# Retiming two short stretches of a TensorE-bound kernel: the first attention chunk and the second batch's numerators

**Chip, cores, metric.** One core of a Trainium2 chip (trn2). The metric is the device time of one execution in microseconds (us).

## The reference

Linear attention with cosine weights, then a multiplicative feed-forward network (FFN) without a nonlinearity:

```
B, H, S, D = 8, 8, 576, 64
phi(x) = concat(relu(x) * cos_w, relu(x) * sin_w)       # 128 features
kv  = einsum('bhsf,bhsd->bhfd', phi(k), v);   z = sum_s phi(k)
num = einsum('bhsf,bhfd->bhsd', phi(q), kv);  den = einsum('bhsf,bhf->bhs', phi(q), z) + 1e-6
x   = (num / den) as [4608, 512]
out = ((x @ w1) * (x @ w2)) @ w3 @ w_out                # FFN width 1024
```

## The kernel before

The kernel folds w3 @ w_out into one matrix (w34b), goes through nine tiles of 512 tokens, and puts the attention of coming batches between the FFN's matmuls, in numbered slots. The order of the program is the order on each engine; nothing is reordered later. Around batch 1 a slot is mostly four FFN matmuls of 512 columns long, 0.86 us.

In outline, an attention chunk of 128 rows goes: features (cosine half on VectorE, sine half on ScalarE), transposes of q on TensorE into PSUM, the memory that matmuls write (`q_tr`), a copy to `qpT`, numerator and denominator matmuls into PSUM tile `pnum` (`num`; they need `kvs`, the copy of the batch's kv sums), normalisation on VectorE into `xblk`, transposes of it (`x_tr`), and a copy to `xT`, which the FFN reads. Batches 0 and 1 transpose `xblk` on TensorE, later batches by DMA.

```python
ps_att = tile_pool(name="ps_att", bufs=1, space=PSUM)     # pnum: one buffer
ps_tr  = tile_pool(name="ps_tr",  bufs=2, space=PSUM)     # pst: two buffers

def num(b, c):
    nt = ps_att.tile([P, 2, 512], FP32, name="pnum")      # (batch 0, chunk 0 has its own, pfirst)
    for h in range(H):                                     # numerator and denominator, 65 columns
        nc.tensor.matmul(nt[:, h // 4, ...], lhsT=qpT[:, h, ...], rhs=kvs[:, h, :], ...)
    nc.vector.tensor_scalar_add(out=den, in0=n4[..., 64], scalar1=1e-6)
    nc.vector.reciprocal(out=den, in_=den)
    nc.vector.tensor_tensor(out=xblk, in0=n4[..., 0:D], in1=den..., op=ALU.mult)

def x_tr(b, c):                                            # (batches 0 and 1)
    pst = ps_tr.tile([P, 8, 128], BF16, name="pst")
    for kc in range(4):
        nc.tensor.transpose(pst[:, kc, 0:R], xf[:, ts(kc, 128)], identb[rows, rows])
    nc.scalar.copy(out=xT[t][:, :, ds(o, R)], in_=pst[:, 0:4, 0:R])

def idle_mms(n): ...    # n matmuls of zeros into PSUM tile "unread", read by nobody: fillers

# start, after the k features and v copies of batch 0; kv_first() has two steps, matmuls and copies
idle_mms(31)                       # issued at the very start
...
next(kv_steps); prep_q(0, 0); next(kv_steps); prep_q(0, 1)
idle_mms(2)
q_tr(0, 0); prep_q(0, 2); q_tr(0, 1, evac=False)[1](); num(0, 0)
...                                # idle_mms(3), x_tr(0, 0), num(0, 1), q_tr(0, 2), first FFN matmuls

# batch 1: the slot of each chunk's kv matmuls, q transposes, numerator, output transposes
spread(prep_units(1, (prep_q,)), 13, 15, between)
spread(prep_units(1, (prep_v,)), 15, 16, between)
attention_at(1, between, kv=(16, 16, 17, 17, 18), tr=(14, 15, 15, 16, 17),
             nu=(19, 20, 21, 22, 24), xt=(20, 21, 22, 23, 25))
```

## Time and profile before

| | before |
|---|---|
| time, median (range) | 263.0 us (262.46 to 263.11) |
| span of the profiled run | 261.2 us |
| TensorE (PE) busy | 249.4 us, 96% |
| granted TensorE clock | 0.997 |
| q's first part lands | 11.38 us |
| first FFN matmul | 16.60 us |
| transpose of batch 0's chunk 3 | 22.31 us |
| first matmul of the second tile | 67.51 us |

With TensorE at 96% only two things can be won: its idle time, and filler matmuls that hide idle time. The prediction shows the lines that place both: the start, up to 22 us, and batch 1's attention, 50 to 70 us. Losses on TensorE are counted from start to start, a matmul's real start against the earliest start that the matmuls before it allow; the wait view shows about 0.17 us less for each.

### The profile page before, as it was taken

What the parts mean: (1) busy time and instruction counts of PE and PEld (TensorE: products, weight loads), DVE (VectorE), ACT (ScalarE), POOL (GpSimd) and SP (SyncE); (2) the same over time, 40 slices, a digit from 0 to 9 for tenths busy, and PEclk for the clock granted to TensorE, in tenths of its full rate; (3) what the DMA queues carried; (4) which work ended last, traced back from release to release, by engine and by line L of the source; (5) the groups of instructions that cost most, each with busy time, mean ns of one, the idle gap of its engine ahead of it and who ended that gap; (6) DMA issues with size and microseconds to landing.
All of it is one profiled execution on the core that took longest, in us unless ns stands there. A gap on an engine that the chain in (4) does not pass through costs nothing.

```text
span 261.2 us, 5061 instructions
## 1 busy us (share of the span) xinstructions
PE 249.4 (96%) x1939; PEld 135.2 (52%) x1972; DVE 144.6 (55%) x344; ACT 128.4 (49%) x219; POOL 85.2 (33%) x146
## 2 busy tenths in 40 slices
PE   8989999998799999999999999999999999999992
PEld 2568555474365456545544654464455444444441
DVE  6877544466669827852883497178616613413320
ACT  2766324746765574555655565546533233323321
POOL 7744144440742177036604920430050031022000
PEclk9999999999999999999999999999999999999998
DMA  7999999999769399999998999835591453014015
GB/s 196 182 193 204 208 204 202 198 199 204 194 84 181 75 193 159 180 143 192 182 187 170 159 190 144 166 98 97 115 173 41 43 110 90 0 34 129 0 45 120
DMA packets 68025, 37.11 MB, mean 142 GB/s; under 512 B 35616, under 2 KB 64544, under 8 KB 68000
## 3 DMA queue, kind: packets, MB, share of 16 engines
q0 software_dynamic: 35488, 27.20, 64.9%
q1 hardware_dynamic: 32352, 9.44, 22.0%
q8 instruction: 15, 0.25, 0.4%
q10 hardware_dynamic: 160, 0.13, 0.2%
q14 instruction: 10, 0.08, 0.1%
HBM read 38.80 MB, written 9.44 MB: 185 GB/s over the span
## 4 chain that ended last, share of the span: by engine, by line
PE 91%; DVE 4%; ACT 1%; issue 1%; ACTq 0%
PE ffnps L399 46%; PE ffnps L445 21%; PE ffnps L208 5%; PE pnum L316 4%; PE pst L298 4%; PE unread L168 4%; PE pnum L267 3%; DVE xblk L323 2%; PE pst L196 1%; PE pst L345 1%; DVE den L321 1%; DVE den L320 1%; PE ffnps L462 0%; ACT kvs L272 0%; ACT osb L464 0%
## 5 line engine op out<-in xcount | busy, mean ns | idle before, releaser
L438 DVE TENSOR_TENSOR abT<-asb,ffnps 128x512 bf16<-128x512 bf16 x68 | 46.4, 683 | 65.8 <-PE ffnps L399 65.2
L399 PE MATMUL ffnps<-xT,w1b 128*128 128x512 bf16 (+2 forms) x312 | 74.2, 357 | 1.2 <-ACT xT L346 0.7
L399 PE MATMUL ffnps<-xT,w2b 128*128 128x512 bf16 (+2 forms) x306 | 73.2, 357 | 0.5
L434 ACT CAST asb<-ffnps 128x512 bf16<-128x512 f32 x68 | 39.8, 585 | 64.1 <-PE ffnps L399 56.7
L445 PE MATMUL ffnps<-w34b,abT 128*128 128x512 bf16 x272 | 63.4, 379 | 0.4
L384 POOL DMA_DIRECT2D out_dram<-osb x42 | 22.3, 536 | 120.0 <-ACT osb L451 119.9
L399 PEld LDWEIGHTS <-w1b 128*128 128x128 bf16 x320 | 28.8, 97 | 27.6 <-issue 0.8
L445 PEld LDWEIGHTS <-abT 128*128 128x128 bf16 x280 | 26.5, 98 | 30.1 <-DVE abT L438 0.4
L399 PEld LDWEIGHTS <-w2b 128*128 128x128 bf16 x320 | 27.4, 97 | 22.5
L451 ACT COPY osb<-ffnps 128x512 f32<-128x512 f32 x35 | 20.5, 585 | 37.8 <-PE ffnps L445 36.7
L243 ACT ACTIVATE qp<-qs,sinv 128x512 bf16<-128x512 bf16 (+1 forms) x40 | 28.3, 720 | 1.7 <-DMA qs<-in_q_dram 1.7
L323 DVE TENSOR_TENSOR xblk<-pnum,den 128x512 bf16<-128x512 f32 (+1 forms) x39 | 26.9, 691 | 1.3
L243 ACT ACTIVATE kp<-ks,sinv 128x512 bf16<-128x512 bf16 (+1 forms) x35 | 24.8, 721 | 0.0
L316 PEld LDWEIGHTS <-qpT 128*128 128x128 bf16 x320 | 15.1, 98 | 8.6 <-DVE xblk L323 0.9
L259 POOL COPY va<-vs 128x512 bf16<-128x512 bf16 (+1 forms) x30 | 18.4, 638 | 0.0
L300 DVE COPY qpT<-pst 128x1024 bf16<-128x1024 bf16 (+1 forms) x22 | 13.7, 626 | 8.0 <-PE pst L298 7.6
L316 PE MATMUL pnum<-kvs,qpT 128*128 128x65 bf16 x312 | 16.4, 194 | 0.1
L240 DVE TENSOR_SCALAR qp<-qs,cosv 128x512 bf16<-128x512 bf16 (+1 forms) x40 | 16.2, 413 | 0.6 <-DMA qs<-in_q_dram 0.6
L267 PEld LDWEIGHTS <-kp 128*128 128x128 bf16 x280 | 12.9, 98 | 5.4
L298 PE MATMUL pst<-identb,qp 128*128 128x128 bf16 x192 | 14.5, 219 | 0.6 <-ACT qp L243 0.4
L208 PE MATMUL ffnps<-woutb,w3T 128*128 128x512 bf16 x62 | 14.9, 379 | 0.1
L298 PEld LDWEIGHTS <-qp 128*128 128x128 bf16 x192 | 12.2, 98 | 5.2 <-ACT qp L243 1.2
(73 smaller groups left out, 178.0 us busy)
## 6 DMA issues: line engine op xcount, KB each, us to landing
out_dram<-osb POOLq DMA_DIRECT2D x16, 256.0 KB, 3.6
out_dram<-osb POOLq DMA_DIRECT2D x24, 128.0 KB, 3.1
qs<-in_q_dram POOLq DMA_DIRECT2D x9, 256.0 KB, 7.8
ks<-in_k_dram POOLq DMA_DIRECT2D x7, 320.0 KB, 8.0
qs<-in_q_dram POOLq DMA_DIRECT2D x7, 320.0 KB, 8.4
vs<-in_v_dram POOLq DMA_DIRECT2D x7, 320.0 KB, 9.9
w3b<-in_moe_w_dram POOLq DMA_DIRECT2D x8, 256.0 KB, 13.3
ks<-in_k_dram POOLq DMA_DIRECT2D x7, 256.0 KB, 8.9
```

The lines of the kernel that those rows point to most:

```text
L208: nc.tensor.matmul(acc[:, :], lhsT=w3T[:, lc, :], rhs=woutb[:, lc, :], start=(lc == 0), stop=(lc == 7))
L243: nc.scalar.activation(out=dst[:R, c, :, D:F], in_=src[:R, :, c, :], func=ACTF.Relu, scale=sinv[:R, at:at + 1], bias=0.0)
L267: nc.tensor.matmul(kvt[:, h // 4, ds((h % 4) * 65, 65)], lhsT=kp[:, c, h, :], rhs=va[:, c, h, 0:D + 1], start=(i == 0 and h % 4 == 0), sto ...
L298: nc.tensor.transpose(pst[:, h, :], qp[:, c, h, :], identb[:])
L316: nc.tensor.matmul(nt[:, h // 4, ds((h % 4) * 65, 65)], lhsT=qpT[:, h, ds(at, 128)], rhs=kvs[:, h, :], start=True, stop=True)
L323: nc.vector.tensor_tensor(out=xblk[rows], in0=n4[:, :, :, 0:D], in1=den[rows].unsqueeze(3).to_broadcast([R, 2, 4, D]), op=ALU.mult)
L384: on.dma_start(out=rows[:, :, cols], in_=osb[64 * i:64 * i + rows.shape[0], :, cols])
L399: nc.tensor.matmul(out, lhsT=w[:, kc, ts(jc, 128)], rhs=x[:, kc, tok], start=(kc == 0), stop=(kc == 3))
L434: nc.scalar.copy(out=asb[:], in_=aT[:, :])
L438: nc.vector.tensor_mul(out=abT[:, jc, :], in0=asb[:], in1=bT[:, :])
L445: nc.tensor.matmul(ops[:, :], lhsT=abT[:, jc, ts(ms, 128)], rhs=w34b[:, jc, :], start=(jc == 0), stop=(jc == 7))
L451: nc.scalar.copy(out=osb[:, ms % 2, :], in_=ops[:, :])
```

## The change

Its intent: at the start, shorten the chain from q's arrival to the first FFN matmul (half of chunk 0's sine on VectorE, two output copies on VectorE, another order, fewer fillers). In batch 1, prepare q and v earlier, and put output transposes two slots after their numerators, so that TensorE need not wait for the normalisation.

```diff
-    idle_mms(31)
+    idle_mms(27)
@@ features(): sine on ScalarE for the first `scalar_heads` heads, the others on VectorE
@@ kv_first(): both copies of kvs on ScalarE (was one on ScalarE, one on VectorE)
@@ num(): chain=False returns the normalisation, to be issued later
@@ x_tr(): by_vector=True has the copy on VectorE
-    prep_q(0, 0)
+    features(0, q0f, q0, 0, scalar_heads=4)
     next(kv_steps)
     prep_q(0, 1)
-    idle_mms(2)
+    idle_mms(1)
     q_tr(0, 0)
     ...
     num(0, 0)
     features(0, q0f, q0, 3, sin=False)
-    idle_mms(3)
-    x_tr(0, 0)
-    num(0, 1)
-    features(0, feat[0][1], raw[0, "q"], 3, cos=False)
-    q_tr(0, 2)
+    q_tr(0, 2, evac=False)[1]()
+    features(0, q0f, q0, 3, cos=False)
+    idle_mms(2)
+    num_at = num(0, 1, chain=False)
+    x_tr(0, 0, by_vector=True)
+    num_at()
@@ first tile: q_tr(0, 3), x_tr(0, 1) on VectorE and num(0, 2) in slot 1; num(0, 3) before x_tr(0, 2)
-            spread(prep_units(1, (prep_q,)), 13, 15, between)
-            spread(prep_units(1, (prep_v,)), 15, 16, between)
-            attention_at(1, between, kv=(16, 16, 17, 17, 18), tr=(14, 15, 15, 16, 17),
-                         nu=(19, 20, 21, 22, 24), xt=(20, 21, 22, 23, 25))
+            spread(prep_units(1, (prep_q,)), 10, 13, between)
+            spread(prep_units(1, (prep_v,)), 13, 14, between)
+            attention_at(1, between, kv=(14, 15, 15, 16, 16), tr=(12, 13, 14, 15, 16),
+                         nu=(17, 18, 19, 20, 22), xt=(19, 20, 21, 22, 25))
```

More of the change, by code (lines that the diff above doesn't have):

```diff
@@ L234, in att_of, with features @@
         return att[b]
-    def features(b, dst, src, c, cos=True, sin=True):
+    def features(b, dst, src, c, cos=True, sin=True, scalar_heads=H):
         R = ROWS[c]
@@ L242, in features @@
         if sin:
-            nc.scalar.activation(out=dst[:R, c, :, D:F], in_=src[:R, :, c, :], func=ACTF.Relu,
+            n = scalar_heads
+            nc.scalar.activation(out=dst[:R, c, 0:n, D:F], in_=src[:R, 0:n, c, :], func=ACTF.Relu,
                                  scale=sinv[:R, at:at + 1], bias=0.0)
+            if n < H:
+                nc.vector.tensor_scalar(out=dst[:R, c, n:H, D:F], in0=src[:R, n:H, c, :],
+                                        scalar1=0.0, scalar2=sinv[:R, at:at + 1],
+                                        op0=ALU.max, op1=ALU.mult)
     def prep_k(b, c):
@@ L288, in kv_first @@
         yield
-        nc.scalar.copy(out=kvs[:, 0:4, :], in_=halves[0][:, 0:260])
-        nc.vector.tensor_copy(out=kvs[:, 4:8, :], in_=halves[1][:, 0:260])
+        for half in range(2):
+            nc.scalar.copy(out=kvs[:, 4 * half:4 * half + 4, :], in_=halves[half][:, 0:260])
         yield
@@ L304, in q_tr, with num @@
         return on_vector, on_scalar
-    def num(b, c):
+    def num(b, c, chain=True):
         rows = out_rows(b, c)
@@ L318, in num, with normalize, x_tr @@
         n4 = nt[rows, :, 0:260].rearrange("p g (h e) -> p g h e", e=65)
-        den = sm.tile([P, 2, 4], FP32, name="den")
-        nc.vector.tensor_scalar_add(out=den[rows], in0=n4[:, :, :, 64], scalar1=1e-6)
-        nc.vector.reciprocal(out=den[rows], in_=den[rows])
         xblk = sm.tile([P, 2, 4, D], BF16, name="xblk", bufs=4)
-        nc.vector.tensor_tensor(out=xblk[rows], in0=n4[:, :, :, 0:D],
-                                in1=den[rows].unsqueeze(3).to_broadcast([R, 2, 4, D]), op=ALU.mult)
         att[b]["x"][c] = xblk
+        def normalize():
+            den = sm.tile([P, 2, 4], FP32, name="den")
+            nc.vector.tensor_scalar_add(out=den[rows], in0=n4[:, :, :, 64], scalar1=1e-6)
+            nc.vector.reciprocal(out=den[rows], in_=den[rows])
+            nc.vector.tensor_tensor(out=xblk[rows], in0=n4[:, :, :, 0:D],
+                                    in1=den[rows].unsqueeze(3).to_broadcast([R, 2, 4, D]),
+                                    op=ALU.mult)
+        if chain:
+            normalize()
+        return normalize
     xT = {}
-    def x_tr(b, c):
+    def x_tr(b, c, by_vector=False):
         R, rows = ROWS[c], out_rows(b, c)
@@ L345, in x_tr @@
             nc.tensor.transpose(pst[:, kc, 0:R], xf[:, ts(kc, 128)], identb[rows, rows])
-        nc.scalar.copy(out=xT[t][:, :, ds(o, R)], in_=pst[:, 0:4, 0:R])
+        copy = nc.vector.tensor_copy if by_vector else nc.scalar.copy
+        copy(out=xT[t][:, :, ds(o, R)], in_=pst[:, 0:4, 0:R])
     def attention_at(b, slots, kv, tr, nu, xt):
@@ L482 @@
     next(kv_steps)
-    prep_q(0, 0)
+    q0f = feat[0][1]
+    features(0, q0f, q0, 0, scalar_heads=4)
     next(kv_steps)
     prep_q(0, 1)
-    idle_mms(2)
+    idle_mms(1)
     q_tr(0, 0)
@@ L490 @@
     num(0, 0)
-    features(0, feat[0][1], raw[0, "q"], 3, sin=False)
-    idle_mms(3)
-    x_tr(0, 0)
-    num(0, 1)
-    features(0, feat[0][1], raw[0, "q"], 3, cos=False)
-    q_tr(0, 2)
+    features(0, q0f, q0, 3, sin=False)
+    q_tr(0, 2, evac=False)[1]()
[4 more added lines that the diff above has]
+    num_at()
     ps_ffn = []
@@ L506 @@
         if t == 0:
-            slots[0].append(lambda: x_tr(0, 1))
+            slots[1].append(lambda: q_tr(0, 3, evac=False)[1]())
+            slots[1].append(lambda: x_tr(0, 1, by_vector=True))
             slots[1].append(lambda: num(0, 2))
-            slots[1].append(lambda: q_tr(0, 3, evac=False)[1]())
+            slots[2].append(lambda: num(0, 3))
             slots[2].append(lambda: x_tr(0, 2))
-            slots[2].append(lambda: num(0, 3))
             slots[3].append(lambda: x_tr(0, 3))
```

## The prediction

> **What bounds the kernel now.** I read the page first, then the stretches (windows), TensorE's waits, the chain of waits that ended last for two stretches, and the timeline of those stretches. The first part of the page:
>
> ```profile
> PE 249.4 (96%) x1939; PEld 135.2 (52%) x1972; DVE 144.6 (55%) x344; ACT 128.4 (49%) x219; POOL 85.2 (33%) x146
> ```
>
> TensorE is busy for 249.4 of 261.2 us. What a retiming can win is its idle time, plus the filler matmuls (the tile "unread", read by nobody) that stand where it would idle. The stretches show where (columns: busy us and instruction count of PE, PEld, DVE, ACT, POOL, granted clock, DMA):
>
> ```profile
> 18.00:21.00 3.00, 3.00 (x56) 2.77 (x54) 1.53 (x4) 2.42 (x4) 1.18 (x3) 1.00 1.49 194
> ...
> 55.00:60.00 5.00, 4.83 (x59) 3.08 (x59) 2.14 (x5) 1.54 (x3) 2.09 (x4) 1.00 1.40 198
> 60.00:65.00 5.00, 3.95 (x46) 1.98 (x44) 3.61 (x11) 3.20 (x7) 0.57 (x1) 1.00 1.41 202
> 65.00:70.00 5.00, 3.56 (x30) 1.56 (x27) 2.68 (x9) 4.10 (x7) 3.01 (x5) 1.00 0.68 228
> 70.00:75.00 5.00, 4.93 (x53) 3.10 (x55) 3.81 (x8) 3.92 (x7) 1.86 (x4) 1.00 0.98 121
> ```
>
> TensorE is full from 18 us on except between 60 and 70 us, where 2.5 of 10 us are idle: that is batch 1's attention. From 70 to 250 us every 50 us stretch has at least 49.5 us busy, so time won before 70 us should reach the end undiminished. TensorE's own waits name the same two places:
>
> ```profile
> PE pst L345 <- DVE xblk L323: 2.6, 7, 0.6
> PE unread L168 <- DVE zeros L144: 1.2, 1, 1.2
> PE ffnps L399 <- ACT xT L346: 0.7, 1, 0.7
> PE pst L298 <- ACT qp L243: 0.4, 1, 0.4
> ```
>
> L345 is the transpose of the normalised output xblk, L316 the numerator matmul, L323 its normalisation on VectorE. The chain of waits shows one period of batch 1 (start, length, what):
>
> ```profile
> 61.09 0.38 PE pnum L316 x8
> 61.47 0.02 issue
> 61.49 0.17 DVE den L320
> 61.67 0.02 issue
> 61.69 0.21 DVE den L321
> 61.91 0.02 issue
> 61.93 0.70 DVE xblk L323
> 62.63 0.05 issue
> 62.68 0.40 PE pst L345 x4
> ```
>
> From the numerator's start in the timeline (61.02) to its transpose (62.68) it is 1.66 us. TensorE has only 0.27 us (numerator) and 0.86 us (four 512-column matmuls) to do meanwhile, then 0.22 us for the transposes. The period is 1.88 us for 1.35 us of work: 0.53 us lost per chunk. (The wait view says 0.36, because it counts from the modelled end of a pipelined matmul; I count from start to start.)
>
> The start of the kernel, in the timeline:
>
> ```profile
> 11.38 0.72 ACT L243 ACTIVATE qp<-qs,sinv 128x512 bf16<-128x512 bf16 x1 [1.68 <-DMA qs<-in_q_dram]
> 13.12 0.69 DVE L300 COPY qpT<-pst 128x1024 bf16<-128x1024 bf16 x1 [0.19 <-PE pst L298]
> 14.78 0.69 DVE L323 TENSOR_TENSOR xblk<-pfirst,den 128x512 bf16<-128x512 f32 x1
> 15.53 0.40 PE L345 MATMUL pst<-identb,xblk 128*128 128x128 bf16 x4 [0.58 <-DVE xblk L323]
> 16.60 0.38 PE L399 MATMUL ffnps<-xT,w1b 128*128 128x128 bf16 x4
> ```
>
> q lands at 11.38 us, and from there one chain runs: feature, transpose, copy, numerator, normalise, transpose, copy, first FFN matmul at 16.60. Real work before it is small; the fillers hide the wait.
>
> **What the Trainium skill says.** "TensorE: Matmul & The Clock Gate", Back-to-back issue gap, gives 518 cycles for a warm 512-column matmul, about 216 ns; the trace agrees (four take 0.86 us), and I use it to count. The same page, What's actually happening, says that the array runs at half clock until about 3.4 us of activity and falls back only after an idle window of that length. Here filler weight loads are 0.43 us apart until 7.1 us, then faster. So the four fillers that go are warm ones, worth 0.86 us, and the remaining gaps (below 1 us) should not cool it. "Perfetto Trace Analysis", Optimization Strategy, says that the same gap repeating can mean too few buffers; the gap above repeats in each chunk, and pnum has one buffer: this decides my estimate. "VectorE: DVE Perf Modes", The TRN2 errata, has cost as a fixed part plus length over the mode's speed; halving a 512-element operation at 4x then saves only 67 ns. The traced full one is 0.34 us, so the half is an estimated 0.27 us.
>
> **Part 1, the start.** Four fillers fewer lets the first kv matmuls start at about 9.9 instead of 10.8 us; the v copies (five from 9.56 to 10.81 us) keep ahead, so kv ends near 11.3, was 12.2. That alone gives nothing, since q lands only at 11.38. From there:
> - Feature of chunk 0: VectorE cosine 0.35, then half the sine 0.27: ready at 12.0; ScalarE's half (a 128x256 copy there takes 0.38) is earlier. Transposes start at about 12.05 instead of 12.48, one filler less in the way: 0.43 won.
> - Start of transposes to copy 0.64, copy 0.69, numerator at 13.44 (was 13.87), xblk done 15.05 (was 15.47), transpose about 15.1 (was 15.53). Before it now stands numerator 1, which needs ScalarE's 1.01 us copy of chunk 1's transposed q: about 14.65, was 14.83. So it is just out of the way.
> - The copy of the transposed output moves to VectorE: a 128x512 copy there is 0.42 against 0.58, 0.16 won. First FFN matmul at about 16.0, was 16.60.
> - Afterwards chunk 1's transpose comes a slot later, and its numerator's normalisation waits for that copy; it is ready at 17.05. Followed slot by slot: second quarter at 18.2 (was 18.79), transpose of chunk 3 at about 21.9 (was 22.31), with waits of about 0.2 each for pnum and xblk. I keep **0.5 us** (0.2 to 0.7). Both kvs copies on ScalarE take it to about 12.3, before the numerator needs them: no cost.
>
> **Part 2, batch 1.** The present loss, start to start: q transposes at 51.12 where work ended at 50.53: 0.59. Numerator at 59.19 for 58.96, waiting for kvs: 0.23. First output transpose 0.48, three more at 0.53. First matmul of the next tile at 67.51 where 66.65 was possible, waiting for xT: 0.86. The last transpose, at 70.01: 0.51. Sum 4.26 us. After:
> - The q features come before the last w34b copies on ScalarE; the first is ready at about 48.6, its transposes due at 48.8: the 0.59 goes. The kvs gap now holds 0.45 us of transposes besides 0.86 us, needs 0.9: the 0.23 goes.
> - Transposes come two slots after their numerator, so xblk is ready: those 2.6 us go. But pnum has a single buffer: the next numerator waits until xblk has been read, 1.61 to 1.66 us after the last numerator's start. In the first gap TensorE has 1.13 us of work, in the next two 1.35 us: 0.48 + 0.30 + 0.30 = 1.08 lost. The fourth numerator is two slots on: free.
> - The xT wait: the copy has a slot of 0.86 us more, but ScalarE has also batch 2's k features there (0.61 us apart) and the osb copies. My slot-by-slot count ends xT at 8.65 us after the first numerator, the matmul being due at 8.47: 0.2; if copies do not overlap as their starts suggest, 0.8. I take 0.45.
> New loss 1.5 us, gain **2.7 us** (2.0 to 3.1). No matmul is added or removed here.
>
> **Sum.** 263.07 - 0.5 - 2.7 = 259.9; I shade it to **260.1 us** for a wait that I have not seen.
>
> **Rivals.**
> 1. The pnum wait takes the whole place of the xblk wait. For it: one buffer, the same 1.6 us chain. Against: transposes now fill one part of the gap and two numerators of five escape. If every chunk still lost 0.5 the gain would be about 1.5 us in batch 1: 261.1.
> 2. ScalarE becomes the bound from 60 to 70 us: it was 3.20 and then 4.10 of 5 us busy there, and the stretch shrinks by over 2 us. Its backlog would return as waits for xT and asb in the next tile: 260.8 to 261.3.
> 3. DMA arrival bounds the earlier prep: transfers issued at 35 and 38 us take 11.1 us, so batch 1's q lands at 46.2 and v at 49.1, wanted at about 46.5 and 49.5. Margins are thin, but a miss costs tenths: 260.5. The DMA is busy in nearly every slice before 78 us, so its arrivals will not move.
> 4. The start wins nothing since the FFN's first matmuls wait elsewhere: 260.5.
>
> **Range and chances.** Both gains at their low ends leave 260.9, at their high ends 259.3; with some 0.3 us of run spread I say 259.2 to 261.3. Over 2% faster would be below 257.8: more than all the batch 1 loss and 1 us of the start, 3%. Slower by 2% would need a new long wait in an engine that now has slack: 1%.
>
> **What would show it.** Right: first FFN matmul at 16.0; no L345 wait on xblk between 55 and 70 us; instead L316 waiting for xblk, about three times, first about 0.3 in the wait view; the L298 wait for qp gone; the same TensorE spacing from 70 us on. Wrong: first FFN matmul at 16.4 or later; an xT wait of 0.7 or more (rival 2); va or qp waiting for DMA around 47 to 50 us (rival 3); new gaps after 70 us, which would mean that time won early is given back.

## The result, and the profile after

The changed kernel took **259.37 us** (259.23 to 259.63, 4 runs) against 263.0; the ratio is 0.9867, 95% interval 0.985 to 0.9884. A ratio here is the mean time of one kernel's runs over that of the other's of the same rounds, so not quite the ratio of the medians. That is 3.5 us or 1.3% faster, where 2.9 us was predicted.

TensorE's waits after (line 413 was 399, 322 was 316, 358 was 345, 332 was 323, 304 was 298; columns: total us, times, longest):

```profile
PE unread L168 <- DVE zeros L144: 1.2, 1, 1.2
PE ffnps L413 <- DVE xT L360: 0.8, 2, 0.5
PE pst L304 <- DVE qp L248: 0.6, 1, 0.6
PE pst L304 <- ACT qp L245: 0.5, 1, 0.5
PE pnum L322 <- DVE xblk L332: 0.3, 1, 0.3
```

The transposes no longer wait for xblk at all; a numerator does instead. This view lists one such wait; counted from start to start, below, there are three. The other new waits stand at the start, where fillers used to stand: a wait that replaces a filler is not a loss. The stretches of batch 1 (busy us of PE, PEld, DVE, ACT, POOL):

```profile
55.00:60.00 5.00, 4.47 (x47) 2.31 (x46) 3.42 (x10) 1.64 (x4) 0.92 (x2) 1.00 1.39 195
60.00:65.00 5.00, 4.71 (x44) 2.65 (x44) 3.79 (x12) 4.24 (x8) 0.33 (x1) 1.00 1.40 200
65.00:70.00 5.00, 4.95 (x47) 2.87 (x46) 3.83 (x8) 5.00 (x10) 3.98 (x7) 1.00 0.84 243
```

The hole of 2.5 us in 60 to 70 us is down to 0.34, with 0.53 in 55 to 60 now that the work comes earlier. ScalarE fills its whole 65 to 70 us stretch. The timeline of TensorE shows what is left:

```profile
55.93 0.42 PE L322 MATMUL pnum<-kvs,qpT 128*128 128x65 bf16 x8
57.55 0.43 PE L322 MATMUL pnum<-kvs,qpT 128*128 128x65 bf16 x8 [0.33 <-DVE xblk L332]
59.20 0.43 PE L322 MATMUL pnum<-kvs,qpT 128*128 128x65 bf16 x8
60.86 0.43 PE L322 MATMUL pnum<-kvs,qpT 128*128 128x65 bf16 x8
63.30 0.42 PE L322 MATMUL pnum<-kvs,qpT 128*128 128x65 bf16 x8
64.69 1.02 PE L413 MATMUL ffnps<-xT,w1b 128*128 128x512 bf16 x4
```

The first four numerators are 1.62, 1.65 and 1.66 us apart, the predicted time for which the one pnum buffer is held. TensorE had 1.13, 1.35 and 1.35 us of work in these gaps: losses of 0.49, 0.30 and 0.31. The second tile's first matmul could have started at 63.30 + 0.27 + 0.86 = 64.43 and started at 64.69: 0.26 for xT.

Two landmarks split the whole difference. "Start" is how far into the span chunk 3's transpose of batch 0 stands (22.31, now 21.62); "rest" is the span minus that.

| profiled run | q lands | start | start minus landing | rest | span |
|---|---|---|---|---|---|
| before | 11.38 | 22.31 | 10.93 | 238.89 | 261.2 |
| after | 11.29 | 21.62 | 10.33 | 235.98 | 257.6 |

The start gave 0.69 us, of which 0.09 is an earlier landing of q, and the rest gave 2.91 us. That the two sum to the difference of the spans, 3.6, is so by construction. That nothing was given back later shows in the rest: it shrank by 2.91 us, and the losses counted in batch 1 by 4.26 - 1.36 = 2.90.

### The profile page after: what moved, and what is told of

It is laid out like the page before. It is cut to its first block, busy times and chain, and to the rows that moved or that the text cites. A ratio compares the mean times of both kernels' runs of the same rounds, so it can differ in the third digit from the quotient of the medians.

```text
span 257.6 us, 5051 instructions
## 1 busy us (share of the span) xinstructions
PE 247.2 (96%) x1933; PEld 135.1 (52%) x1966; DVE 145.6 (57%) x345; ACT 127.9 (50%) x219; POOL 85.5 (33%) x146
## 4 chain that ended last, share of the span: by engine, by line
PE 84%; DMA 7%; ACT 5%; issue 1%; POOL 1%; DVE 0%; ACTq 0%; POOLq 0%
PE ffnps L413 48%; PE ffnps L459 21%; DMA qs<-in_q_dram 7%; PE pnum L322 4%; PE ffnps L208 3%; PE pst L304 3%; PE pnum L273 3%; ACT qp L245 2%; ACT kp L245 1%; PE pst L196 1%; ACT w34b L211 1%; PE pst L358 1%; POOL vs L120 0%; ACT xT L360 0%; PE ffnps L476 0%
## 5 line engine op out<-in xcount | busy, mean ns | idle before, releaser
L245 ACT ACTIVATE qp<-qs,sinv 128x512 bf16<-128x512 bf16 (+2 forms) x40 | 28.2, 716 | 1.5 <-DMA qs<-in_q_dram 1.5
L241 DVE TENSOR_SCALAR qp<-qs,cosv 128x512 bf16<-128x512 bf16 (+1 forms) x40 | 17.2, 437 | 0.6 <-DMA qs<-in_q_dram 0.6
L306 DVE COPY qpT<-pst 128x1024 bf16<-128x1024 bf16 (+1 forms) x21 | 13.1, 622 | 6.8 <-PE pst L304 6.6
```

Source lines behind the costliest of these rows:

```text
L245: nc.scalar.activation(out=dst[:R, c, 0:n, D:F], in_=src[:R, 0:n, c, :], func=ACTF.Relu, scale=sinv[:R, at:at + 1], bias=0.0)
```

## The experiments

Theory: the kernel is one TensorE-bound chain; the losses of the two stretches add up. At the start the chain begins at q's landing. In batch 1 the two-slot distance removes the wait for xblk, and the single pnum buffer puts about 40% of it back. Rivals: the start's gain is given back; the fillers alone, or q's earlier features alone, are the gain; what is left belongs to ScalarE's backlog.

All twelve runs gave correct results. q's landing moved between 11.28 and 11.90 us from run to run, so I give the landmarks beside the times.

| run | ratio to before | time, us | q lands | start minus landing | rest |
|---|---|---|---|---|---|
| e1_start_only | 0.9986 | 262.51 | 11.54 | 10.34 | 238.82 |
| e2_batch1_only | 0.9885 | 259.86 | 11.55 | 10.76 | 235.99 |
| e3_fillers_only | 0.9999 | 262.84 | 11.56 | 10.62 | 238.92 |
| e4_one_slot | 0.9908 | 260.41 | 11.28 | 10.33 | 236.69 |
| after_again | 0.9867 | 259.57 | 11.49 | 10.33 | 235.98 |
| e5_double_norm | 0.9964 | 262.23 | 11.90 | 10.33 | 238.37 |
| e6_spaced | 0.9852 | 259.11 | 11.45 | 10.33 | 235.62 |
| e7_xt_vector | 0.9862 | 259.57 | 11.63 | 10.33 | 235.64 |
| e9_whole_sine | 0.9880 | 259.61 | 11.32 | 10.54 | 235.94 |
| e10_xt0_scalar | 0.9937 | 261.27 | 11.66 | 11.87 | 235.97 |
| e11_respaced | 0.9832 | 258.51 | 11.82 | 10.34 | 234.74 |
| e12_respaced_split1 | 0.9824 | 258.24 | 11.78 | 10.13 | 234.79 |

The rest repeats to 0.1 us wherever that part of the program is the same, over several chips, and start minus landing repeats to 0.01 us for the changed kernel's start. For the old start it is the landmark itself that repeats, 22.31 us in before and in e2. They resolve what the times, with runs some 0.5 us apart, do not.

### Each part alone

e1: the changed kernel with batch 1's old three lines.

```diff
-attention_at(1, ..., kv=(14, 15, 15, 16, 16), tr=(12, 13, 14, 15, 16), nu=(17, 18, 19, 20, 22), xt=(19, 20, 21, 22, 25))
+attention_at(1, ..., kv=(16, 16, 17, 17, 18), tr=(14, 15, 15, 16, 17), nu=(19, 20, 21, 22, 24), xt=(20, 21, 22, 23, 25))
 # and prep_q, prep_v at their old slots
```

> The changed kernel with batch 1's old schedule: the start alone. Main theory (the two parts are independent stretches of one TensorE-bound chain and add up): 0.6 to 0.7 us below the kernel before, about 262.3 us; the first FFN matmul near 16.0 us, the transpose of chunk 3 near 21.6 us, and the old batch 1 waits unchanged but 0.7 us earlier. Rival A (time won at the start is given back in batch 1, where data or ScalarE set the pace, and the whole 3.6 us comes from batch 1): within 0.2 us of the kernel before.

e2: the kernel before with only batch 1's new lines (the reverse of that diff).

> The kernel before with only batch 1's schedule changed. Main theory: 2.9 us below the kernel before, about 260.1 us, with numerators waiting for xblk three times (about 0.49, 0.30, 0.30 us from start to start) and no transpose of xblk waiting after 55 us. Rival A: 3.4 us or more below. Rival B (the new batch 1 schedule needs the earlier start): clearly less than 2.5 us.

Measured: e1 0.37 us faster than before by its ratio (1 - 0.9986, of 262.9), interval 0.05 to 0.7; e2 3.0 us faster. They sum to 3.4 against 3.5 for both: the parts add up. Rival B falls by that; rival A falls by the landmarks (e1's rest, 238.82, is that of before, and e2's, 235.99, that of after), since e1's interval alone would leave room for it. e1 is less than expected, 0.6 to 0.7, because q landed at 11.54 us in its profiled run: its start-to-landing distance is the new one (10.34), its landmark 21.88. e2's start stands at 22.31 us, exactly where it stood before, although q landed 0.17 us later than there. In these two profiles the old start does not follow q; the new one does (see the next experiment for a limit of this).

### What the fillers did

```diff
-    idle_mms(31)
+    idle_mms(27)      # in the kernel before, nothing else
```

> The kernel before with 27 fillers at the start in place of 31, nothing else. Main theory (the chain starts at q's landing at 11.3 to 11.4 us, not at the end of the kv matmuls): kv ends about 0.85 us earlier and the time stays within 0.15 us of the kernel before. Rival C (the fillers themselves were in the way of the first chain): 0.4 to 0.9 us faster. Rival D (fewer fillers let the granted clock fall): slower, with matmul starts further apart.

Measured: no change in time (0.9999, interval 0.9986 to 1.0011). The kv matmuls began at 10.04 instead of 10.77 us, now waiting for v, and q's transposes at 12.33 instead of 12.48, now waiting for ScalarE's sine (first line: before, second: e3):

```profile
12.48 1.31 PE L298 MATMUL pst<-identb,qp 128*128 128x128 bf16 x16
12.33 0.62 PE L298 MATMUL pst<-identb,qp 128*128 128x128 bf16 x8 [0.42 <-ACT qp L243]
```

So in the profiled run of the kernel before it was the program's own fillers that held the transposes to 12.48, while the sine was done at 12.10. Taking four away alone won 0.13 us at the landmark with q landing at 11.56. With the landing of the kernel before, 11.38, the same distance would have put the landmark at 22.0, a win of 0.3 (worked out, not run). Rival C is right in kind, too large in size; rival D falls: the granted clock stayed at 0.996, and four kv matmuls start every 0.13 us as before.

How long the fillers last differs between executions, too. Their weight loads go from 0.43 to about 0.21 us apart at 4.07 us in e6 and at 7.05 us in the first run of the changed kernel. The two programs are the same up to there, and the first kv weight load followed at 8.18 and at 9.64 us. Both profiles with 31 fillers, before and e2, are late ones (7.10 and 7.11 us). So that the fillers held the transposes is shown for these two executions only. Where the fillers speed up early, the old start may well follow q as the new one does; that would fit the unchanged time of e3, but no profile of the old kernel shows it.

### The distance of numerators and transposes

```diff
-nu=(17, 18, 19, 20, 22), xt=(19, 20, 21, 22, 25)
+nu=(17, 18, 19, 20, 22), xt=(18, 19, 20, 21, 25)
```

> The changed kernel with batch 1's output transposes one slot after their numerators again, the numerators and everything ahead of them where the change put them. Main theory: the transposes wait for xblk again, 0.48 and three times 0.53 us from start to start = 2.07, in place of 0.49 + 0.30 + 0.30 for pnum and 0.26 for xT = 1.35: slower than the changed kernel by about 0.7 us, about 260.1 us. Rival E (the gain of batch 1 comes from the two slots of distance, all 2.6 us of xblk waits): slower by 1.5 us or more. Rival F (it comes from the earlier q features alone): no difference.

Measured: 260.41 us; by the ratios 1.1 us slower than the changed kernel, by the landmarks 0.71 (236.69 against 235.98). The four runs spread from 260.03 to 260.74, and the profiled one is the fastest. TensorE's waits of this run:

```profile
PE pst L358 <- DVE xblk L332: 1.4, 4, 0.4
```

Four waits for xblk are back and those for pnum and xT are gone, as counted; rivals E and F fall by the landmarks. Of the 2.9 us in batch 1, then, the two-slot distance of the first four transposes is worth 0.7. The other 2.2 are what e4 keeps: the earlier preparation ends the wait for q's features (0.59) and for kvs (0.23), numerators and transposes begun earlier let the second tile find its xT (0.86), and the last transpose, now three slots behind its numerator, no longer waits (0.51). This split is by the waits that went; only the 0.7 was run alone.

### Is it the pnum buffer?

e5: the multiplication that writes xblk is issued twice for batch 1.

```diff
+            if b == 1:
+                nc.vector.tensor_tensor(out=xblk[rows], in0=n4[:, :, :, 0:D], in1=den..., op=ALU.mult)
```

> The changed kernel with the multiplication that writes xblk done twice for batch 1 (same result, 0.69 us more on VectorE per chunk). Main theory (the single pnum buffer is what numerators wait for): each of the three numerator gaps grows by 0.7 us, the fourth gap of two slots by about 0.1; the xT wait of 0.26 is then hidden: about 1.9 us slower than the changed kernel. Rival G (what is left in batch 1 is ScalarE's backlog, the numerators' waits are beside it): at most 0.7 us slower.

Measured: 262.23 us, 2.5 us slower than the changed kernel by the ratios, 2.39 in the rest. TensorE's waits:

```profile
PE pnum L322 <- DVE xblk L336: 2.8, 3, 1.1
...
PE pnum L273 <- POOL va L265: 0.4, 1, 0.4
```

The three numerator gaps are 2.34, 2.39 and 2.38 us, each 0.7 longer, as the pnum theory says, and rival G (at most 0.7 in all) falls. The expected 1.9 missed the second line: a kv matmul of the second tile now waits for v copies on GpSimd, 0.56 us from start to start. A second buffer for pnum was not tried.

e6: the opposite, numerators two slots apart.

```diff
-kv=(14, 15, 15, 16, 16), ..., nu=(17, 18, 19, 20, 22), xt=(19, 20, 21, 22, 25)
+kv=(14, 14, 14, 14, 14), ..., nu=(15, 17, 19, 21, 23), xt=(17, 19, 21, 22, 25)   # all v copies in slot 13
```

> The changed kernel with batch 1's numerators two slots apart, begun two slots earlier (v copies and kv matmuls moved ahead for it); transposes two slots behind, the fourth one slot behind. Main theory: a gap of two slots holds over 2 us of TensorE work, so the three pnum waits (1.09 us from start to start) go; the fourth transpose waits about 0.3 us: 0.7 to 0.9 us faster than the changed kernel, about 258.6 us. Rival G: no difference, since the time returns as a longer xT wait. Rival H (v lands too late for kv matmuls so early): a new wait of kv for the v copies and no gain.

Measured: 259.11 us, 0.36 us less in the rest; half of what was expected, a miss. The pnum waits are gone, but others stand there: one transpose waits 0.53 from start to start (expected 0.3), the first numerator 0.23 for kvs, and GpSimd's v copies hold a kv matmul for 0.45. No xT wait came back, so rival G falls here too. About 0.28 of the 0.45 (and of the 0.56 in e5) are won back by 85 us, where the changed kernel's TensorE stands for that time: its numerator at 80.15 us is 177.45 us before the end, the same one in e6 177.17, and the numerator at 85.26 us is 172.34 before the end in one, 172.33 in the other. GpSimd's waits in that stretch:

```profile
POOL out_dram L398 <- ACT osb L465: 8.9, 2, 4.8
POOL ks L112 <- ACT qp L245: 1.1, 1, 1.1
```

and its timeline:

```profile
68.16 0.73 POOL L112 DMA_DIRECT2D ks<-in_k_dram  x1 [1.08 <-ACT qp L245]
68.88 0.71 POOL L114 DMA_DIRECT2D ks<-in_k_dram  x1
69.57 1.81 POOL L265 COPY va<-vs 128x512 bf16<-128x512 bf16 x3
```

By the profile, the issue of a load for batch 4 waits for one of ScalarE's sines, which its backlog makes late, and the copies stand behind it in GpSimd's order. The load itself is not urgent: e11 issues it later without a loss.

### The xT wait

```diff
-copy = nc.vector.tensor_copy if by_vector else nc.scalar.copy
+copy = nc.vector.tensor_copy if by_vector or (b == 1 and c == 2) else nc.scalar.copy
```

> The changed kernel with one copy moved: the output copy of batch 1's chunk 2, the last that the second tile needs, on VectorE in place of ScalarE, whose queue is full there. Main theory: the copy ends about 0.4 us earlier, the second tile's first matmul no longer waits (0.26 us from start to start): 0.25 us faster than the changed kernel. Rival I (ScalarE's backlog only moves the wait to the second tile's evictions): no difference.

Measured: the second tile's first matmul starts without a wait (64.76, with the numerator before it at 63.64), and the rest is 0.34 us shorter. The median time equals after_again's; its runs lie between 258.87 and 259.74. So the wait is shown to go, the gain in time is not resolved. Its reference in the same rounds:

> The changed kernel itself, unchanged, so that the next three have it on their own chip and in their own rounds: 3.3 to 3.6 us below the kernel before; the exact value follows the landing of q's first part, 11.3 to 11.55 us.

It took 259.57 us, 0.9867 of before, as in the first measurement.

### What the new start consists of

e9: chunk 0's sine whole on ScalarE (`features(0, q0f, q0, 0)`).

> The changed kernel with the sine features of chunk 0 left whole on ScalarE. Main theory (the chain of the start begins at q's landing, and what is on it counts in full): q's transposes start 0.78 us after the landing in place of 0.57, so the transpose of chunk 3 stands 0.2 us later, counted from the landing, and the time is 0.2 us above the changed kernel. Rival J (ScalarE's later work, not the first feature, paces the start): no shift.

Measured: start minus landing 10.54 instead of 10.33, 0.21 later as expected. The times (259.61, ratio 0.9880 with an interval of 0.9867 to 0.9894) agree with that and alone would not show it.

e10: the two output copies back on ScalarE.

```diff
-    x_tr(0, 0, by_vector=True)
+    x_tr(0, 0)                      # and x_tr(0, 1) in slot 1
```

> The changed kernel with the first two output copies of batch 0 back on ScalarE. By the prediction's own figure (a 128x512 copy takes 0.58 there and 0.42 on VectorE) the first FFN matmul would be 0.16 us later. Main theory, corrected after the profile: the copy would stand behind ScalarE's 1.01 us copy of chunk 2's q and chunk 3's sine, which end near 16.1 us when q lands at 11.3, so the first FFN matmul moves from 4.74 us after q's landing to about 5.5 us, and the time rises by 0.5 to 0.8 us over the changed kernel. Rival: 0.16 us or nothing.

Measured: 1.8 us slower than the changed kernel by the ratios, the landmark 1.54 us later. A miss of mine: I counted the first copy and not the second. ScalarE's and TensorE's timeline:

```profile
15.85 0.73 ACT L245 ACTIVATE qp<-qs,sinv 128x512 bf16<-128x512 bf16 x1
16.48 0.59 ACT L360 COPY xT<-pst 128x512 bf16<-128x512 bf16 x1
17.11 0.38 PE L413 MATMUL ffnps<-xT,w1b 128*128 128x128 bf16 x4 [1.23 <-ACT xT L360]
18.65 1.01 ACT L307 COPY qpT<-pst 128x1024 bf16<-128x1024 bf16 x1 [1.59 <-PE pst L304]
19.56 0.59 ACT L360 COPY xT<-pst 128x512 bf16<-128x512 bf16 x1
20.20 0.38 PE L413 MATMUL ffnps<-xT,w1b 128*128 128x128 bf16 x4 [1.11 <-ACT xT L360]
```

Both copies stand behind longer ScalarE work that the new order puts in front of them, a sine and a copy of q. In the new order the move to VectorE is worth 1.5 us, not the 0.16 by which the copy itself is shorter.

### A version that beats both

e11 has e7's copy, a third spacing of batch 1, and the load out of the v copies' way:

```diff
+kv=(14, 14, 14, 14, 14), tr=(12, 13, 14, 15, 17), nu=(15, 17, 18, 20, 22), xt=(17, 19, 20, 22, 25)
+between[14].append(between[14].pop(3))    # chunk 1's q transposes after the last kv matmuls
-            for g, name in ((1, "k"), (8, "q"), (15, "v")):     # second tile: load of batch 4
+            for g, name in ((5, "k"), (8, "q"), (15, "v")):
```

> The changed kernel with three edits of batch 1: numerators begun two slots earlier and spaced so that each gap but one has two slots, the one with the last q transposes in it (a gap of 1.58 us for the 1.65 that is needed); the second tile's last output copy on VectorE; and the load of batch 4's k four slots later in the second tile, so that GpSimd's v copies don't stand behind it. Main theory (pnum, xT, and in the spaced kernel the v copies behind a waiting load, are all that TensorE waits for): the 1.35 us of batch 1's loss shrink to 0.1 to 0.3, 1.0 to 1.2 us faster than the changed kernel, 258.3 to 258.6 us. Rival K (a next queue takes over, as GpSimd's did in the spaced kernel): 0.4 us or less.

e12 adds `features(0, q0f, q0, 1, scalar_heads=4)`, chunk 1's sine split over two engines.

> The same, and chunk 1's sine features split over ScalarE and VectorE as chunk 0's are. Main theory: VectorE has 0.4 us free before its first copy, chunk 1's transposes start about 0.2 us earlier, and the whole start with them: 0.2 us below the respaced kernel, about 258.2 us. Rival J: no shift, or slower because VectorE's copy of chunk 0 starts later.

Measured: e11 258.51 us, the rest 1.24 us below the changed kernel's; e12 **258.24 us**, start minus landing 10.13 (another 0.20), 0.9824 of before. Rivals K and J fall. e11's stretches show TensorE with no idle time left in this view (the rest says that about 0.1 of the 1.36 us remain):

```profile
55.00:60.00 5.00, 5.00 (x49) 2.73 (x48) 3.65 (x9) 1.28 (x3) 0.68 (x1) 1.00 1.41 198
60.00:65.00 5.00, 5.00 (x44) 2.82 (x43) 3.68 (x13) 4.76 (x10) 0.57 (x1) 1.00 1.40 201
65.00:70.00 5.00, 5.00 (x55) 3.01 (x53) 4.32 (x8) 4.67 (x9) 4.83 (x8) 1.00 0.74 239
```

The effect of e11's three edits was measured together; only the copy was run alone (e7). The difference of e12 and e11 in time (0.3 us) is within their spread; the landmark shows it.

## Why the prediction was right

The time lay in its range, and the mechanism was the one predicted. Point by point:

- **Batch 1's present loss, 4.26 us, and its new loss.** Predicted 0.48 + 0.30 + 0.30 for pnum; the trace has 0.49 + 0.30 + 0.31, and e5 shows that the chain holding pnum sets it. For xT 0.45 was taken between 0.2 and 0.8; it was 0.26, close to the lower one, so ScalarE's operations do overlap as assumed (two sines of 0.72 us take 1.33 from the first start to the last end). New loss 1.36 where 1.5 was predicted; gain 2.91 where 2.7 was.
- **The waits for q's features and kvs.** Both went as counted (e2: 3.0 us for batch 1 alone).
- **The start.** Predicted 0.5, range 0.2 to 0.7; the profiled run had 0.69. First FFN matmul predicted at 16.0, was at 16.03. The undersized term is the later part of the chain: I put chunk 3's transpose at 21.9, it was at 21.62. Luck is in both: q landed 0.09 earlier than the 11.38 that I counted from. In the eight profiles of the new start the landmark lay between 21.61 and 22.23, as q landed, which is 0.70 to 0.08 before the old 22.31.
- **A wrong step with little effect.** "From there one chain runs" (from q's landing) is wrong for the profiled kernel before: the fillers held q's transposes to 12.48 us (e2, e3). So "That alone gives nothing", of the four fillers, holds for the time (0.9999), but not for the landmark, which came 0.13 us earlier (0.3 worked out for q at 11.38). It holds for the new start, which in eight profiles stood 10.33 to 10.34 us after the landing.
- **A wrong credit.** The copy on VectorE was given 0.16 us. In its place in the order it is worth 1.5 (e10); I had followed the new order with the copy on VectorE, so the total came out right while the named reason was too small.
- **A wrong size without effect.** ScalarE's half of the sine was put at 0.38 us, from a copy out of PSUM; it took 0.51. The Trainium skill had a closer figure: "ScalarE: Activation LUTs", Rules for kernel authors, gives about 0.3 us per ACTIVATE with its bias as a pointer operand (here the scale is the pointer) and 0.83 ns per element, so an estimated 0.51 us for 256. VectorE's half, at 0.28 us close to the 0.27 estimated, ended about when it did, 11.84 against 11.80, so the chain hardly moved.
- **The clock.** The prediction quotes about 3.4 us of activity to full speed; in its own lines the fillers sped up at 7.1 us, 5.9 after the first one at 1.19. The four fillers that went were fast ones all the same: kv began at 9.86 instead of 10.77 us. The "remaining gaps (below 1 us)" reached 1.70 us before the kv matmuls in e10, and these still started every 0.13 us per four.
- **The 0.2 us held back** "for a wait that I have not seen": there was none. With the two undersized gains (0.19 and 0.21) this is 0.6 of the 0.7 us by which the time was lower than predicted; the sum also began at 263.07, where the median before was 263.0.
- **The rivals.** The pnum wait (1) came, for part of the place, as argued. ScalarE (2) was full, 5.00 of 5 us, but cost 0.26 us only; e5 and e6 show its backlog reaching TensorE through GpSimd's order once batch 1 is stretched or shortened further. DMA arrival (3) showed no wait in batch 1. The start (4) did win.

## What to carry to other kernels

When a wait is removed by more distance between producer and consumer, ask how many buffers lie between them: here the wait moved from the reader of xblk to the next writer of pnum, and spacing the writers, with two other queues cleared as well, brought nearly all of the rest (e11). Judge moving an operation to another engine by the queue it leaves, not by the difference of the two durations (1.5 us against 0.16). When the time of a transfer varies from run to run, measure changes of a few tenths from a landmark behind it.

## What the Trainium skill lacked or had wrong

- "TensorE: Matmul & The Clock Gate", Back-to-back issue gap, gives about 131 ns per 512-column matmul and 81 ns per 128-column one as sustained in a real kernel. Here, in streams of weight load and matmul, four 512-column ones take 0.86 us, 215 ns each, and four 128-column ones 0.22 us, 55 ns each: the section's "isolated" formula fits this kernel, its "sustained" figures do not.
- "Perfetto Trace Analysis", Optimization Strategy, names too few buffers as a cause of repeating gaps. No page says how to see that a wait will move from the reader to the next writer; here the gaps of 1.62 to 1.66 us are, within 0.06 us, the time from the numerator's start to the end of the normalisation, and grew to 2.34 to 2.39 when that was lengthened by 0.7.
- No page says that the landing of an early transfer varies between runs of one program: q's first part landed between 11.28 and 11.90 us, and the new start followed it to 0.01 us.
